# Prologue and chunk 0 of an attention and feed-forward kernel in another order

## The chip, the cores and the metric

One core of a Trainium2 chip runs the whole kernel in one launch. The metric is the device time in microseconds (us) from the start to the end of one execution, as the median of several runs.

## The reference, cut to what matters

Eight batches of 576 tokens go through attention with eight heads of 64 columns, and the result through a normalised feed-forward layer with a residue. Heads 0 to 3 are "local": a token sees the 32 tokens up to itself, within a band. Heads 4 to 7 are "strided": a token sees earlier tokens with the same position modulo 32.

```python
scores = scale * np.matmul(q, k.transpose(0, 1, 3, 2))
scores = np.where(masks[None], scores, -1e9)
attn = softmax(scores)
x = (attn @ v) as [8, 576, 512]
xn = (x - mean) / sqrt(var + 1e-6) * g_ln
out = x + np.maximum(xn @ w_ch1, 0) @ w_ch2
```

w_ch1 is 512 by 2048 and w_ch2 is 2048 by 512. Everything is float32.

## The kernel before, in words

**Chunks and steps.** The feed-forward layer runs over nine chunks of 512 tokens (chunk c is the first 512 tokens of batch c, the ninth holds the 64 left over from each batch). A chunk is 16 steps f, one for each 128 of the 2048 hidden columns. A step is F and H (12 matmuls of 128 by 512, with the weights and the input each split into a high and a low part, lines 758 and 765), hh and hl (the rectified result split, lines 770 and 775) and G (12 matmuls into the output, line 785). From chunk 1 on, attention for the next batch is mixed in between.

**Weights.** The weights arrive as float32 and are split in chunk 0, once, and stay. W:f loads step f's two weight tiles of 512 KB (lines 227 and 230). Then, for tile i of step f: sc scales (ScalarE), low or lowA takes the low bits out (VectorE or ScalarE), mg and sg put the rounded value together (VectorE), and hi (ScalarE) and lo (POOL, or VectorE with the letter D) make the high and low parts. For the first tile there stand in between: byg, a product with g_ln (POOL), add, a sum of blocks (POOL), cm, a matmul that gives column means (line 284), and cen, their subtraction (VectorE).

**Attention in the prologue and chunk 0.** A pair is two heads of one batch. Pairs 0 to 3 are batch 0, pairs 4 to 7 are batch 1; even ones are strided, odd ones local. For a pair k below 5: R:k:1 and R:k:0 load the rows of k and of q (two loads of 144 KB each; with a last field of 1, one of the two goes out on ScalarE's queue), T:k:1 and T:k:0 turn them with six transposes each (line 371), c copies the result out of PSUM (ScalarE, or VectorE as cD), S makes the scores (line 443), mask and max (VectorE), sub (POOL, or VectorE as subD), exp (ScalarE), PP turns the weights (line 499), pt copies them (ScalarE, or VectorE as ptD), V multiplies with the values (line 512), den and xo divide (VectorE), X turns the result for the layer (line 633), xh and xl split it. v:k loads the values, vs:k shifts a copy of them on POOL for a local pair. From pair 5 on, r:k loads 128-byte pieces of q and k in another layout and tp:k turns them on VectorE. Fp and Hp are step 0's F and H, one pair at a time (line 851). g loads g_ln as four rows, gt turns it on TensorE into the tile "wake", gc copies it out (lines 870 to 874). st:k stores a pair's result, xr and xs load the residue and its statistics.

**Order.** Chunk 0 and everything ahead of it is written out by hand as a list of such words, ORDER (from line 20). Each engine and each queue runs its own instructions in just that order: the last lines of the kernel add a dependency from each instruction to the one before it on its engine. So a word that waits holds up every later word of its engine. The last field of a word of TensorE is one of three PSUM buffers (room). SyncE's queue carries all loads and stores named above, but for the halves on ScalarE's queue; each load waits until an earlier one that used its semaphore is back, eight can be out. The words Z and Y are known to the function that runs the list, but the list before has none:

```python
elif op in "ZY":
    t = room(f"d{k}", buf) if op == "Y" else wake
    nc.tensor.matmul(
        t[:, 0:CH].rearrange("p (n x) -> p n x", x=P), mean.bitcast(F32R),
        mean.bitcast(F32R).unsqueeze(1).broadcast_to([P, CH // P, P]),
        start=True, stop=True)
```

They multiply a constant with itself into a buffer that nobody reads. Ahead of the list, six such products of 128 columns are run on TensorE (line 126).

The head of the list before V:4 on TensorE, without the other engines, is: T:0:0 T:0:1 T:1:1 T:1:0 S:0 S:1 T:2:1 T:2:0 PP:0 S:2 PP:1 V:0 T:3:1 gt T:3:0 X:0 S:3 T:4:1 V:1 T:4:0 cm:0 PP:2 S:4 X:1 PP:3 V:2 V:3 Fp:1 X:2 cm:1 Hp:0 Fp:0 Hp:1 X:3 Hp:2 PP:4 Fp:2 Fp:3 Hp:3 cm:2 S:5 V:4, then F:1 H:1 G:0 and so on.

Of the kernel before, what the change touches and what calls it, by code (L numbers as in the profile page):

```python
# [17 lines left out]


ORDER = """  # L20
vm R:0:1:1 R:0:0:1 R:1:1:1 T:0:0:0 R:1:0:1 T:0:1:1 cD:0:0: T:1:1:2 cD:1:1: T:1:0:0 c:0:1: S:0::2
R:2:1 R:2:0 W:0 c:1:0: v:0 mask:0 max:0 sub:0 S:1::0 T:2:1:1 T:2:0:2 c:2:1: mask:1 max:1 exp:0 R:3:1
PP:0::0 cD:2:0: low:0:0 sc:0:0 S:2::2 mg:0:0 sub:1 mask:2 exp:1 pt:0 sg:0:0 PP:1::0 pt:1 V:0::1
max:2 R:3:0 g:0 sc:0:1 sub:2 T:3:1:2 v:1 den:0 xo:0 gt:0: gc:0: T:3:0:0 low:0:1 c:3:1: c:3:0: X:0::2
R:4:1 byg:0 mg:0:1 vs:1 sg:0:1 xh:0 R:4:0 S:3::1 xl:0 hi:0:1 T:4:1:0 W:1 c:4:1: v:3 lo:0:1 mask:3
exp:2 max:3 sc:1:0 V:1::2 v:2 T:4:0:0 add:0 W:2 cm:0::1 den:1 c:4:0: xo:1 low:1:0 r:5 PP:2::2
lowA:1:1 mg:1:0 cen:0 pt:2 sub:3 sg:1:0 sc:1:1 S:4::0 X:1::2 mask:4 exp:3 mg:1:1 byg:1 xh:1 max:4
vs:3 hi:0:0 PP:3::1 pt:3 xl:1 lowA:2:0 V:2::0 V:3::2 sg:1:1 den:2 lo:0:0 Fp:1 sc:2:0 add:1 xo:2
X:2::0 cm:1::1 v:4 den:3 Hp:0 Fp:0 lowA:2:1 mg:2:0 Hp:1 xo:3 sub:4 hi:1:1 sg:2:0 cen:1 xh:2 W:3
exp:4 X:3::2 lo:1:1 byg:2 xl:2 xh:3 Hp:2 W:4 PP:4::1 Fp:2 hi:1:0 xl:3 st:1 Fp:3 add:2 pt:4 tp:5  # L30
sc:2:1 Hp:3 cm:2::0 mg:2:1 hh:0 cen:2 S:5::2 hl:0 hi:2:0 V:4::0 sg:2:1 lowA:3:0 mask:5 lo:1:0 den:4
sc:3:0 lo:2:0 mg:3:0 hi:2:1 sg:3:0 lowA:3:1 F:1 W:5 H:1 byg:3 xo:4 sc:3:1 hh:1 mg:3:1 sg:3:1 add:3
G:0 lowA:4:0 hl:1 sc:4:0 mg:4:0 sg:4:0 hi:3:1 cm:3::0 lo:2:1 cen:3 F:2 lowA:4:1 sc:4:1 hi:3:0 lo:3:1
lo:3:0 mg:4:1 lowA:5:0 H:2 sg:4:1 max:5 hh:2 X:4::0 sc:5:0 hl:2 G:1 byg:4 mg:5:0 F:3 sg:5:0 sub:5
add:4 xh:4 lowA:5:1 W:6 xl:4 sc:5:1 cm:4::0 lowA:6:0 hi:4:1 byg:5 mg:5:1 lo:4:1 sg:5:1 add:5
lowA:6:1 sc:6:0 st:2 H:3 G:2 W:7 cen:4 mg:6:0 sg:6:0 hi:4:0 hh:3 hi:5:1 byg:6 sc:6:1 hl:3 cm:5::0
exp:5 lo:4:0 F:4 mg:6:1 add:6 lowA:7:0 H:4 sg:6:1 low:7:1 sc:7:0 cen:5 cm:6::0 hi:6:1 G:3 mg:7:0
sg:7:0 cen:6 byg:7 hi:5:0 sc:7:1 mg:7:1 hh:4 r:6 W:8 sg:7:1 hl:4 st:0 hi:7:1 lowA:8:0 PP:5::0 lo:5:0
F:5 pt:5 H:5 tp:6 sc:8:0 lo:7:1 st:3 mg:8:0 S:6::0 sg:8:0 hi:6:0 hh:5 G:4 v:5 W:9 lowA:8:1 lo:6:1
add:7 loD:5:1 hl:5 sc:8:1 lo:6:0 mask:6 mg:8:1 st:4 max:6 cm:7::0 sg:8:1 hi:8:1 sc:9:0 subD:6 W:10  # L40
F:6 H:6 cen:7 loD:8:1 V:5::0 exp:6 byg:8 G:5 low:9:0 hh:6 hi:7:0 W:11 r:7 mg:9:0 sg:9:0 lowA:9:1
sc:9:1 add:8 den:5 hl:6 byg:9 lowA:10:0 xo:5 cm:8::0 mg:9:1 sg:9:1 addD:9 hi:9:1 sc:10:0 lo:7:0
cen:8 F:7 low:10:1 hi:8:0 H:7 mg:10:0 W:12 lo:9:1 sg:10:0 PP:6::0 hh:7 sc:10:1 hl:7 lo:8:0 mg:10:1
pt:6 lowA:11:1 lowA:11:0 G:6 cm:9::0 sg:10:1 sc:11:0 cen:9 mg:11:0 byg:10 F:8 hi:9:0 add:10 W:14
hi:10:1 sg:11:0 cm:10::0 cen:10 H:8 sc:11:1 mg:11:1 hi:10:0 byg:11 lo:10:1 hh:8 lo:9:0 add:11 tp:7
sg:11:1 G:7 hl:8 lowA:12:0 sc:12:0 mg:12:0 W:13 lo:10:0 S:7::0 lowA:12:1 mask:7 sg:12:0 F:9 sc:12:1
lowA:14:0 hi:11:1 max:7 H:9 cm:11::0 mg:12:1 cen:11 byg:12 hh:9 add:12 sg:12:1 lo:11:1 sc:13:0 G:8
st:5 cm:12::0 hl:9 hi:11:0 low:13:0 lo:11:0 hi:12:1 mg:13:0 lowA:13:1 sg:13:0 v:6 sc:13:1 sub:7
lowA:14:1 F:10 cen:12 H:10 mg:13:1 sg:13:1 hi:12:0 X:5::0 hh:10 W:15 xh:5 loD:12:0 G:9 xl:5 sc:14:0
hl:10 mg:14:0 hi:13:1 byg:13 exp:7 V:6::0 sg:14:0 lo:12:1 sc:14:1 xr:2 add:13 F:11 den:6 xo:6 H:11  # L50
lowA:15:1 xs:2 mg:14:1 hh:11 xr:1 lo:13:1 cm:13::0 G:10 cen:13 hi:13:0 xr:0 sg:14:1 sc:15:0
lowA:15:0 hl:11 hi:14:1 X:6::0 F:12 xs:1 xh:6 mg:15:0 byg:14 xs:0 r:8 H:12 lo:13:0 sg:15:0 sc:15:1
addD:14 G:11 lo:14:1 hh:12 xl:6 st:6 hl:12 cm:14::0 F:13 byg:15 mg:15:1 xr:3 add:15 cen:14 H:13
PP:7::0 G:12 tp:8 ptD:7 v:7 v:8 hi:14:0 hh:13 cm:15::0 lo:14:0 hl:13 F:14 H:14 sg:15:1 cen:15
hi:15:1 hi:15:0 lo:15:1 hh:14 V:7::0 r:9 lo:15:0 den:7 hl:14 G:13 xo:7 xs:3 X:7::0 F:15 H:15 xh:7
st:7 hh:15 xl:7 hl:15 G:14
"""
# [1011 lines left out]
```

## Time and profile before

| what | value |
|---|---|
| median of 3 runs | 897.91 us (897.63 to 898.39) |
| the profiled execution, its own time | 899.09 us |
| its span, first to last instruction | 897.3 us |
| TensorE busy | 880.3 us, 98% |
| VectorE, ScalarE, POOL busy | 451.0, 197.3, 143.2 us |
| mean granted clock of TensorE | 0.992 |
| moved by DMA | 103.74 MB |

A profile is one execution. PE is TensorE's matmul, DVE is VectorE, ACT is ScalarE, SPq is SyncE's queue that issues transfers. A window row gives, for a stretch of the execution, how long each engine was busy in it and the clock that TensorE was granted, as a share of full speed. A timeline row gives start, duration, engine, line of the kernel, operation and shapes; x24 means that 24 like instructions in a row were merged; the bracket gives the idle time of the engine before it and what ended it. Times count from the start of the span.

### The profile page before, as it was taken

What the parts mean: (1) busy time and instruction counts of PE and PEld (TensorE: products, weight loads), DVE (VectorE), ACT (ScalarE), POOL (GpSimd) and SP (SyncE); (2) the same over time, 40 slices, a digit from 0 to 9 for tenths busy, and PEclk for the clock granted to TensorE, in tenths of its full rate; (3) what the DMA queues carried; (4) which work ended last, traced back from release to release, by engine and by line L of the source; (5) the groups of instructions that cost most, each with busy time, mean ns of one, the idle gap of its engine ahead of it and who ended that gap; (6) DMA issues with size and microseconds to landing.
All of it is one profiled execution on the core that took longest, in us unless ns stands there. A gap on an engine that the chain in (4) does not pass through costs nothing.

```text
span 897.3 us, 18263 instructions
## 1 busy us (share of the span) xinstructions
PE 880.3 (98%) x7453; PEld 725.1 (81%) x7453; DVE 451.0 (50%) x883; ACT 197.3 (22%) x321; POOL 143.2 (16%) x178
## 2 busy tenths in 40 slices
...
GB/s 188 180 293 268 256 112 101 128 163 124 114 143 145 111 113 136 125 112 113 126 128 113 112 91 147 127 107 103 144 121 69 38 118 11 1 1 94 1 1 47
DMA packets 352683, 103.74 MB, mean 116 GB/s; under 512 B 295124, under 2 KB 344408, under 8 KB 352600
## 3 DMA queue, kind: packets, MB, share of 16 engines
...
q14 instruction: 25, 0.20, 0.1%
...
## 4 chain that ended last, share of the span: by engine, by line
PE 94%; DMA 2%; DVE 2%; issue 1%; SPq 1%; POOL 0%; ACT 0%; ACTq 0%; DVEq 0%; POOLq 0%
PE po L785 43%; PE ph L758 28%; PE ph L765 14%; PE m L512 2%; PE m L443 2%; PE s L443 1%; PE t L371 1%; PE pp L499 1%; PE av L512 1%; DMA rows<-in_q_dram 1%; DMA rows<-in_k_dram 0%; DMA pt<-pd 0%; DMA v_s<-in_v_dram 0%; SPq L399 0%; PE cm L284 0%
## 5 line engine op out<-in xcount | busy, mean ns | idle before, releaser
L785 PE MATMUL po<-w,hh 128*128 128x512 f32 x1152 | 359.0, 393 | 0.0
L775 DVE SCALAR_TENSOR_TENSOR hl<-ph,hh 128x512 fp32r<-128x512 f32 x144 | 99.4, 690 | 351.1 <-ACT hh L770 351.0
L785 PEld LDWEIGHTS po<-w,hh 128*128 128x128 f32 x1152 | 213.5, 188 | 45.3
L785 PE MATMUL po<-w,hl 128*128 128x512 f32 x576 | 224.5, 390 | 0.0
L758 PE MATMUL ph<-xh,w 128*128 128x512 f32 x572 | 224.0, 392 | 0.0
L758 PE MATMUL ph<-xl,w 128*128 128x512 f32 x572 | 222.7, 389 | 0.0
L770 ACT ACTIVATE hh<-ph 128x512 fp32r<-128x512 f32 x144 | 86.0, 597 | 465.1 <-PE ph L765 425.9
L765 PE MATMUL ph<-xh,w 128*128 128x512 f32 x572 | 153.2, 390 | 0.0
L785 PEld LDWEIGHTS po<-w,hl 128*128 128x128 f32 x576 | 108.1, 188 | 22.8
L758 PEld LDWEIGHTS ph<-xh,w 128*128 128x128 f32 x572 | 107.4, 188 | 22.3
L765 PEld LDWEIGHTS ph<-xh,w 128*128 128x128 f32 x572 | 107.2, 188 | 22.3
L758 PEld LDWEIGHTS ph<-xl,w 128*128 128x128 f32 x572 | 107.4, 188 | 22.0
L489 POOL TENSOR_TENSOR sm<-sm,mx 128x640 f32<-128x640 f32 (+1 forms) x31 | 39.4, 1270 | 343.1 <-DVE mx L484 343.1
L719 POOL TENSOR_TENSOR rs<-rs,mhalf 128x1 f32<-128x1 f32 x36 | 19.8, 550 | 357.2 <-DVE rs L718 357.1
L495 ACT ACTIVATE sm<-sm 128x648 f32<-128x648 f32 (+1 forms) x32 | 23.8, 744 | 108.2 <-POOL sm L489 108.2
L683 DVE TENSOR_TENSOR xl<-xo,xh 128x512 fp32r<-128x512 f32 x28 | 19.4, 693 | 40.0 <-ACT xh L682 40.0
L301 POOL TENSOR_TENSOR w<-r,w 128x512 fp32r<-128x512 f32 x29 | 38.0, 1320 | 8.3 <-ACT w L297 6.4
L682 ACT ACTIVATE xh<-xo 128x512 fp32r<-128x512 f32 x28 | 17.7, 632 | 69.1 <-DMA raw<-in_q_dram 24.8
L484 DVE TENSOR_REDUCE mx<-sm 128x12 f32<-128x648 f32 (+1 forms) x32 | 26.3, 823 | 2.5
L562 DVE TENSOR_TENSOR xo<-m,den 64x64 f32<-64x64 f32 (+3 forms) x120 | 27.1, 290 | 0.0
L791 DVE SCALAR_TENSOR_TENSOR x<-po,rs,x 128x512 f32<-128x512 f32 x36 | 24.6, 739 | 2.3 <-PE po L785 2.2
L714 DVE BATCH_NORM_STATS2 st<-x 128x6 f32<-128x512 f32 x36 | 24.5, 682 | 0.0
...
## 6 DMA issues: line engine op xcount, KB each, us to landing
...
raw<-in_q_dram SPq DMA_DIRECT2D x108, 72.0 KB
raw<-in_k_dram SPq DMA_DIRECT2D x108, 72.0 KB
...
```

The lines of the kernel that those rows point to most:

```text
L301: eng.tensor_tensor(out=t[:, 1], in0=self.w[i], in1=t[:, 0].bitcast(F32), op=ALU.subtract)
L443: nc.tensor.matmul(o, lhsT, rhs, start=True, stop=True, tile_position=(64 * h, pos))
L484: nc.vector.reduce_max(mx[:, :, 0:nt], sm, axis=AX.X)
L489: eng.tensor_tensor(out=sm, in0=sm, in1=mx[:, :, 0:nt].unsqueeze(3).broadcast_to([P, 2, nt, sm.shape[3]]), op=ALU.subtract)
L512: nc.tensor.matmul(at(h, t)[m * j:m * (j + 1)], self.p_cols(rows, t, j), self.v[rows, n, 0:w], start=True, stop=True, tile_position=(64 * ...
L562: nc.vector.tensor_tensor(out=xo[r, t0:t1, h0:h1].rearrange("p t h d -> p h t d"), in0=av, in1=den[r, h0:h1, t0:t1].unsqueeze(3).broadcast_to(
L758: nc.tensor.matmul(ph, w1h[:, cc], x[:, cc, :], start=(new and n == 0 and i == 0), stop=False)
L765: nc.tensor.matmul(ph, w1l[:, cc], xt[c][0][:, cc, :], start=False, stop=(cc == NCC - 1))
L770: nc.scalar.activation(out=hh, in_=ph, func=AF.Relu)
L775: nc.vector.scalar_tensor_tensor(out=hl, in0=ph, scalar=0.0, in1=hh.bitcast(F32), op0=ALU.max, op1=ALU.subtract)
L785: nc.tensor.matmul(po[i], hx[:, cs], w, start=(f == 0 and n == 0), stop=(f == NFC - 1 and n == 2))
L791: nc.vector.scalar_tensor_tensor(out=x, in0=po[i], scalar=rs, in1=x, op0=ALU.mult, op1=ALU.add)
```

## The change

Only the list ORDER is changed. Nothing else is touched. The head of it, with "-" the list before and "+" the list after:

```diff
-vm R:0:1:1 R:0:0:1 R:1:1:1 T:0:0:0 R:1:0:1 T:0:1:1 cD:0:0: T:1:1:2 cD:1:1: T:1:0:0 c:0:1: S:0::2
-R:2:1 R:2:0 W:0 c:1:0: v:0 mask:0 max:0 sub:0 S:1::0 T:2:1:1 T:2:0:2 c:2:1: mask:1 max:1 exp:0 R:3:1
-PP:0::0 cD:2:0: low:0:0 sc:0:0 S:2::2 mg:0:0 sub:1 mask:2 exp:1 pt:0 sg:0:0 PP:1::0 pt:1 V:0::1
-max:2 R:3:0 g:0 sc:0:1 sub:2 T:3:1:2 v:1 den:0 xo:0 gt:0: gc:0: T:3:0:0 low:0:1 c:3:1: c:3:0: X:0::2
-R:4:1 byg:0 mg:0:1 vs:1 sg:0:1 xh:0 R:4:0 S:3::1 xl:0 hi:0:1 T:4:1:0 W:1 c:4:1: v:3 lo:0:1 mask:3
-exp:2 max:3 sc:1:0 V:1::2 v:2 T:4:0:0 add:0 W:2 cm:0::1 den:1 c:4:0: xo:1 low:1:0 r:5 PP:2::2
...
+vm R:0:1:1 g:0 R:0:0:1 gt:0: R:1:1:1 T:0:1:1 T:0:0:2 R:1:0:1 T:1:1:0 W:0 gc:0: c:0:1: cD:0:0: c:1:1:
+S:0::1 mask:0 Y:0::0 Y:1::2 T:1:0:1 R:2:1 max:0 sub:0 lowA:0:0 sc:0:0 cD:1:0: mg:0:0 sg:0:0 S:1::0
+R:2:0 T:2:1:2 lowA:0:1 byg:0 T:2:0:1 exp:0 sc:0:1 mask:1 v:0 c:2:1: PP:0::0 mg:0:1 max:1 R:3:1 add:0
+sg:0:1 R:3:0 c:2:0: ptD:0 sub:1 hi:0:1 v:1 S:2::1 mask:2 V:0::2 T:3:1:0 exp:1 c:3:1: lo:0:1 den:0
+xo:0 PP:1::1 max:2 pt:1 T:3:0:2 X:0::0 c:3:0: cm:0::1 R:4:1 R:4:0 subD:2 exp:2 S:3::2 vs:1 cen:0 W:1
+xh:0 PP:2::1 xl:0 T:4:1:0 mask:3 max:3 hi:0:0 pt:2 v:3 low:1:0 lo:0:0 T:4:0:1 v:2 Hp:0 Fp:0 sub:3
+c:4:1: sc:1:0 c:4:0: lowA:1:1 V:1::2 mg:1:0 sg:1:0 den:1 S:4::0 xo:1 W:2 byg:1 r:5 exp:3 mask:4
...
```

On SyncE's queue the order of loads was R:0:1 R:0:0 R:1:1 R:1:0 R:2:1 R:2:0 W:0 v:0 R:3:1 R:3:0 g v:1 R:4:1 R:4:0 W:1 v:3 v:2 W:2 r:5 v:4 W:3 W:4 st:1 W:5 W:6. It becomes R:0:1 g R:0:0 R:1:1 R:1:0 W:0 R:2:1 R:2:0 v:0 R:3:1 R:3:0 v:1 R:4:1 R:4:0 W:1 v:3 v:2 W:2 r:5 v:4 W:3 W:4 W:5 W:6 st:1.

On TensorE the head becomes: gt T:0:1 T:0:0 T:1:1 S:0 Y:0 Y:1 T:1:0 S:1 T:2:1 T:2:0 PP:0 S:2 V:0 T:3:1 PP:1 T:3:0 X:0 cm:0 S:3 PP:2 T:4:1 T:4:0 Hp:0 Fp:0 V:1 S:4 X:1 PP:3 cm:1 Hp:1 V:2 V:3 X:2 Fp:1 X:3 PP:4 Hp:2 Hp:3 Fp:2 Fp:3 cm:2 S:5 V:4, then F:1 H:1 G:0 and so on.

The two products Y:0 and Y:1 are new. Over the whole list some words change engine: of the copies c one more is ScalarE's (8 instead of 7), of the low bits two more (27 instead of 25), of sub one more is VectorE's (2 instead of 1), of add one fewer (1 instead of 2). In the part after F:1 the words stand a few places earlier or later; so S:6 goes between F:5 and H:5, PP:7 between F:13 and H:13, V:7 between F:14 and H:14, V:5 behind G:5.

## Rows read from the trace of the kernel before

**Rows 1.** Windows of the whole execution: stretch, its length, each engine's busy time, granted clock
```profile
core 0: us, PE busy (x) PEld busy (x) DVE busy (x) ACT busy (x) POOL busy (x), PEclk, DMA share, GB/s
0.00:47.74 47.74, 37.18 (x828) 31.35 (x828) 34.61 (x72) 26.79 (x40) 29.98 (x57) 0.89 0.97 191
...
30.89:46.76 15.87, 14.86 (x309) 12.06 (x309) 13.01 (x24) 12.50 (x21) 11.60 (x12) 0.81 0.76 162
47.74:143.15 95.41, 95.41 (x764) 78.14 (x760) 83.63 (x138) 58.55 (x101) 65.10 (x66) 1.00 0.86 222
```

**Rows 2.** Timeline of PE: start, duration, engine, line, operation, shapes, count, [idle before <- releaser]
```profile
24.64 0.69 PE L371 MATMUL t<-ident,rows 96*128 96x96 f32 x6 [0.29 <-DMA rows<-in_k_dram]
...
26.90 0.47 PE L371 MATMUL t<-ident,rows 96*128 96x96 f32 x3
30.89 0.74 PE L371 MATMUL t<-ident,rows 96*128 96x96 f32 x3 [3.53 <-issue]
...
44.77 0.38 PE L284 MATMUL cm<-bsum,mean 128*128 128x128 f32 x2
45.63 1.03 PE L443 MATMUL s<-kt_l,qt_l 64*32 64x64 f32 x80 [0.48 <-DVE kt_l L414]
46.76 1.05 PE L512 MATMUL av<-v_s,pt 54*64 54x65 f32 x48
47.74 0.50 PE L758 MATMUL ph<-xh,w 128*128 128x512 f32 x1
```

**Rows 3.** Windows around PE's gaps, columns as in rows 1
```profile
14.40:16.06 1.66, 0.00 (x1) 0.01 (x1) 1.56 (x4) 1.62 (x3) 1.18 (x2) 1.00 0.91 141
16.40:19.70 3.30, 3.30 (x58) 2.74 (x56) 2.46 (x5) 1.57 (x3) 0.57 (x1) 0.51 1.22 186
...
30.40:36.80 6.40, 5.91 (x68) 5.25 (x68) 3.56 (x6) 4.55 (x7) 3.17 (x3) 0.50 0.86 222
36.80:46.76 9.96, 8.95 (x242) 6.80 (x241) 9.86 (x20) 7.95 (x15) 8.43 (x10) 0.99 0.67 119
...
45.00:47.74 2.74, 2.16 (x131) 1.84 (x129) 2.74 (x5) 1.20 (x2) 1.09 (x2) 1.00 0.92 302
```

**Rows 4.** Timeline of SyncE's queue from 0 to 60 us
```profile
4.67 0.86 SPq L364 DMA_DIRECT2D rows<-in_k_dram  x2
...
7.79 1.21 SPq L227 DMA_DIRECT2D s<-in_moe_w_ch_dram  x1
...
17.01 0.60 SPq L870 DMA_DIRECT2D grow<-in_moe_g_ln_dram  x1
...
31.29 0.40 SPq L227 DMA_DIRECT2D s<-in_moe_w_ch_dram  x1
...
41.31 2.38 SPq L399 DMA_DIRECT2D v_s<-in_v_dram  x6
```

**Rows 5.** DMA: 36 to 46 us in 40 slices, then packets of 45 to 46, 46 to 47
```profile
GB/s 235 199 161 130 120 96 80 93 23 10 43 183 145 22 64 170 51 7 10 5 0 81 172 83 181 124 65 82 108 153 127 129 132 157 127 104 91 86 105 296
...
DMA packets 162, 0.14 MB, mean 145 GB/s; under 512 B 27, under 2 KB 162, under 8 KB 162
...
DMA packets 346, 0.37 MB, mean 369 GB/s; under 512 B 7, under 2 KB 339, under 8 KB 346
```

**Rows 6.** Timelines of ScalarE and VectorE
```profile
27.67 0.63 ACT L247 ACTIVATE p<-s 128x512 f32<-128x512 f32 x1 [0.52 <-DMA s<-in_moe_w_ch_dram]
...
15.47 1.23 DVE L382 COPY qt_s<-t 128x576 f32<-128x576 f32 x1
16.53 0.72 DVE L257 TENSOR_SCALAR s<-s 128x512 uint32<-128x512 uint32 x1
...
44.73 0.76 DVE L414 STREAM_TRANSPOSE kt_l<-raw 128x576 f32<-128x576 f32 x1
...
78.94 0.83 DVE L489 TENSOR_TENSOR sm<-sm,mx 128x648 f32<-128x648 f32 x1
```

**Rows 7.** DMA queues from 27 to 31 us
```profile
q8 instruction: 1, 0.02, 2.0%
```

More of the change, by code (lines that the diff above doesn't have):

```diff
@@ L26 @@
-exp:2 max:3 sc:1:0 V:1::2 v:2 T:4:0:0 add:0 W:2 cm:0::1 den:1 c:4:0: xo:1 low:1:0 r:5 PP:2::2
[L27 to L55, printed above, removed]
@@ L56 @@
-st:7 hh:15 xl:7 hl:15 G:14
+vm R:0:1:1 g:0 R:0:0:1 gt:0: R:1:1:1 T:0:1:1 T:0:0:2 R:1:0:1 T:1:1:0 W:0 gc:0: c:0:1: cD:0:0: c:1:1:
[3 more added lines that the diff above has]
+xo:0 PP:1::1 max:2 pt:1 T:3:0:2 X:0::0 c:3:0: cm:0::1 R:4:1 R:4:0 subD:2 exp:2 S:3::2 vs:1 cen:0 W:1
@@ new lines @@
+xh:0 PP:2::1 xl:0 T:4:1:0 mask:3 max:3 hi:0:0 pt:2 v:3 low:1:0 lo:0:0 T:4:0:1 v:2 Hp:0 Fp:0 sub:3
+c:4:1: sc:1:0 c:4:0: lowA:1:1 V:1::2 mg:1:0 sg:1:0 den:1 S:4::0 xo:1 W:2 byg:1 r:5 exp:3 mask:4
+X:1::2 add:1 PP:3::0 sc:1:1 mg:1:1 cm:1::1 xh:1 vs:3 max:4 pt:3 Hp:1 sg:1:1 sub:4 cen:1 V:2::0
+hi:1:1 V:3::1 sc:2:0 xl:1 lowA:2:0 den:2 xo:2 mg:2:0 lo:1:1 X:2::2 exp:4 v:4 den:3 Fp:1 hi:1:0 xo:3
+xh:2 sg:2:0 lo:1:0 W:3 lowA:2:1 byg:2 X:3::1 PP:4::0 xh:3 xl:2 add:2 sc:2:1 W:4 xl:3 Hp:2 Hp:3 pt:4
+Fp:2 Fp:3 mg:2:1 tp:5 hh:0 cm:2::0 S:5::1 sg:2:1 cen:2 hl:0 W:5 V:4::0 mask:5 F:1 hi:2:1 den:4 H:1
```

25 lines of the change are left out of this document (added).

## The prediction

> **What bounds the kernel now.** I read the windows of the profile first, by stage. From 47.74 us, where TensorE (PE) starts the first full step of chunk 0 (F:1), to 143.15, where chunk 1 begins, PE is busy 100% at a clock of 1.00 [rows 1]. The change keeps every matmul behind F:1 and only permutes them inside chunk 0, so this part can lose by a new wait but has no idle time to give back. What is open to gain is the prologue: 37.18 us busy of 47.74 [rows 1]. The order of words before V:4 holds the same set in both orders, apart from the two products Y, so the end moves by as much as F:1 moves, plus any new stall or slow clock behind it.
>
> The second view is the timeline of PE. It shows the idle times: 1.66 us before PP:0 [rows 3], 3.53 in the middle of the six transposes of T:4:0 (three run at 26.90, three at 30.89, all on the same rows, released by "issue", so not by data), 0.48 before S:5 [rows 2]. The tempting reading is that these waits, and the two stretches at half clock behind two of them (0.51 from 16.40 to 19.70, 0.50 from 30.40 to 36.80, [rows 3]), are the prize. The third view, SyncE's queue with the DMA rows, speaks against it. W:2 was issued at 31.29, then r:5, then v:4 from 41.31 for 2.38 us [rows 4]. V:4 reads v:4's rows, which go in pieces under 512 B; of these 27 stand between 45 and 46 us and 7 between 46 and 47, where W:3's larger pieces already dominate [rows 5]. So the last of v:4 lands at about 46.2 to 46.5, and V:4 ran at 46.76 [rows 2]: the prologue ends 0.3 to 0.6 us behind its loads. Upstream it is alike: T:4:1 waited 0.29 us for R:4 [rows 2], ScalarE 0.52 us for W:1, up to 27.67 [rows 6].
>
> **The change, part by part.**
> *Loads.* SyncE's order changes in two places: g (2 KB, at 17.01) goes to second place, and W:0's two issues (from 7.79) go ahead of R:2's four (from 4.67) [rows 4]. From v:0 on to W:4 the list is the same, and the bytes ahead of each load are the same but for g. g saves the queue 0.60 us in the middle [rows 4] and takes one place among the first loads, so half of R:1's q rows goes out later, on ScalarE's queue. It still stands behind loads in flight, and T:1:0, its reader, now comes after S:0, so I cost it at nothing; without that cover T:1:0, S:1 and T:2 slip, and T:4:1's load still ends the slip. R:2 lands later by W:0's 1 MB: at the rate of such pieces, 0.37 MB in the microsecond from 46 [rows 5], 2.8 us. So T:2 slips by up to that. What is late next is S:2, but V:0, T:3 and T:4 behind it wait for loads that have not moved (T:4:1 at 24.64), so the delay ends there. Price for v:4's landing: 0, between -0.6 (g's issue) and +0.6 (the slot).
>
> *The two products* of 512 columns: the first matmul of F:1, of that size, took 0.50 us [rows 2], so 1.0 us for both at full clock, up to 2.0 at half. They stand between S:0 and T:1:0, ahead of the wait for T:4:1, so they cost nothing at the end; without that cover 2 us.
>
> *Engines.* One copy of pair 2's rows moves from VectorE to ScalarE, both low-bit operations of step 0 likewise; sub:2 moves from POOL and pt:0 from ScalarE to VectorE. VectorE, which was busy 9.86 of the 9.96 us before V:4 [rows 3], gives away 1.2 + 2 x 0.7 us and takes 2 x 0.8 (rows of such forms: 1.23, 0.72 and 0.83, [rows 6]; pt:0 is put at sub's), so 1.0 us less. It transposed r:5's keys at 44.73 [rows 6], the release of S:5. r:5's last issue lies before 41.31; v:4's last, at 43.7, is back 2.5 to 2.8 us later, so by the same delay r:5 is in by 43.4 to 43.9, or sooner, and S:5, one 0.76 us transpose later, can go to about 44.2, 1.4 us earlier. That helps only up to V:4's data. ScalarE has more to do ahead of S:4: the copy c:4:0 stands behind sc:1:0, which waits for W:1, as it did at 27.67; S:4 comes at about 29.7, behind W:1 by one scaling and one copy, well ahead of V:4.
>
> *PE between T:4:0 and V:4.* Before: 14.86 us busy from 30.89 to 46.76 [rows 1], of it 5.91 at half clock [rows 3]; at full clock that is 14.86 - 2.95 = 11.9. After, cm:0, PP:2 and half of T:4:0 are done earlier (1.2 us) and V:1 comes later (1.0): 11.7. T:4:0 needs R:4's last half, between 24.64 and 26.90 by rows 2; I take 26.9 for its end. So 11.7 us of work stand in the 19.3 us up to 46.2: PE will idle some 7.6 us there, waiting for W:1, v:2, W:2, r:5 and v:4, whose order is unchanged. The stall at T:4:0 is not saved, it is spread.
>
> *Sum.* F:1 goes from 47.74 to about 47.3: -0.4 (bounds -0.6 and 0). Then the clock. After 1.66 us without a matmul the granted clock was 0.51 (the 1.2 GHz level) for the next 3.3 us; after 3.53 us it was 0.50 for 6.4 us [rows 3]. In the new order PE has S:5 alone (1.03 us) between cm:2 and V:4 at 46.2. cm:2 ran at 44.77 [rows 2]; I put it 2 us earlier, 42.8, an estimate: VectorE, which feeds it, has 1.0 us less to do and PE's gap of 3.53 us is no longer in front. That leaves 2.4 us idle, in two pieces, just ahead of the dense steps. So I expect one half-clock stretch to reach into V:4 and F:1. A whole one of 3.3 us costs 1.65; if it starts up to 1.3 us before V:4, 1.0. I take 1.3. Sum: -0.4 + 1.3 = +0.9 us, on the profiled execution 897.3 to 898.2 of span. That execution took 899.09 us in all, 1.18 above the median of the three runs, 897.91; the difference goes on top of the median: 898.8.
>
> A short gap did not have this effect: behind 0.48 us at 45.63 [rows 2] the clock stayed at 1.00 [rows 1, 3]. The Trainium skill, "TensorE: Matmul & The Clock Gate", section "HAM oscillation — how this bites in real kernels", says that a TensorE that waits for DMA between bursts of matmuls is throttled again and starts the next burst cold, at half rate. That rule speaks against an order that turns one gap into several; taken for every gap here it would give the third rival below, 900.7, where the rows of short gaps alone would give the first, 897.5.
>
> **The rivals.**
> *Clock holds:* the idle time falls in pieces too short, or S:5 keeps the clock up. For it: the 0.48 us gap left it at 1.00. Against it: the 1.66 us gap. -0.4: 897.5.
> *Loads come sooner (faster):* between 38.0 and 41.25 ten of thirteen slices of the GB/s row stand at 64 or less, although k rows of r:5 and all of v:4 were still to come [rows 5]. If that hole, 2.5 us, follows from what else sits in the queues at that moment (an instruction packet, say, like that of [rows 7]), another timing may close it. VectorE and PE are ready by then, S:5 and V:4 move up by 2.5, F:1 to 45.2: 895.4. Against it: the loads in front are the same.
> *Clock stays down (slower):* as from 30.40 to 36.80 [rows 3]: 6.4 us at half, 3.2 lost if all of it falls on V:4 and the dense steps, less 0.4: +2.8, 900.7. It decides if the 2.4 us idle ahead of V:4 act like the gap of 3.53 us rather than like that of 1.66; they lie between.
> *Stall at the same place in PE's program:* one packet of the instruction queue stands in the stretch of the 3.53 us gap [rows 7]. If it was the release, the gap returns at the same count of instructions, now in V:1, up to 30.9. S:4 then comes at 31, and V:2 behind it waits for v:2 until about 33.5 anyway (its issue ends at 31.29, [rows 4]). It changes nothing at the end, so it is part of the forecast.
>
> **How the numbers follow.** About 0.2%, 1.8 us, is what a measurement can tell. Forecast (one slow stretch, 898.8): 0.40, range of its own 898.3 to 899.6 from the bounds (-0.6 + 1.0 and 0 + 1.65). Clock holds (897.5): 0.22, also within 0.2%. Loads sooner (895.4): 0.18, faster. Clock stays down (900.7): 0.16, slower. A new wait inside chunk 0, where VectorE is busy 83.63 of 95.41 us [rows 1] and a permuted word could be late: 0.04, slower, 901 and more. So faster 0.18, same 0.62, slower 0.20. The range reaches from the case of sooner loads to a little above that of the clock that stays down, 895.3 to 901.0.
>
> **What would show it.** Right: T:4:1 waits for R:4 at 24 to 25 us; no 3.5 us gap, but several gaps of 0.5 to 1.7 us from 27 to 46; S:5 near 44, V:4 near 46.3, F:1 near 47.3; granted clock near 0.5 somewhere from 44 to 50; 100% busy from F:1 on. Wrong: v:4's small pieces ending before 45 or F:1 before 46.5 (loads were not the bound), or idle PE between F:1 and chunk 1.

## The result, and the profile after

The new order is slower: 904.23 us (median of four runs, 902.63 to 905.39) against 897.85 for the kernel before (897.63 to 898.39), a ratio of 1.0069 with a 95% interval of 1.0051 to 1.0086. That lies outside the predicted range. The profiled execution took 902.63 us, with a span of 900.82; the profiled one of before had a span of 897.3. So the traces show 3.5 of the 6.4 us; the other three runs of the kernel after have no trace.

The windows of the kernel after (columns as in rows 1) say where to look. F:1 starts at 47.14, chunk 1 at 147.85:

```profile
0.00:47.14 47.14, 35.58 (x830) 29.39 (x830) 33.92 (x72) 28.98 (x43) 29.20 (x56) 0.96 0.99 189
47.14:80.00 32.86, 32.54 (x197) 25.86 (x193) 31.48 (x48) 25.47 (x44) 27.79 (x30) 1.00 0.98 292
80.00:110.00 30.00, 30.00 (x293) 24.50 (x292) 26.64 (x42) 20.59 (x35) 24.49 (x26) 1.00 0.92 261
110.00:147.85 37.85, 34.35 (x277) 27.63 (x276) 24.41 (x45) 12.97 (x22) 12.38 (x15) 1.00 0.57 106
```

The prologue ends 0.60 us sooner, near the 0.4 of the forecast. From F:1 on, where PE was busy 95.41 of 95.41 us [rows 1], it now idles 3.50 us behind 110 and 0.32 ahead of 80, at a granted clock of 1.00. From F:1 to chunk 1 it takes 100.71 us, 5.30 more than before; 3.82 of them are these idle times, the rest stands between matmuls, in time that counts as busy. No slow clock is in this: the half-clock stretch lay earlier, from 40 to 44 us (0.55, 0.50, 0.50 and 0.74 in its four microseconds), behind a gap of 2.02 us, and was over by 44. The rows that answer to rows 2 and 3, from the timeline of PE and from windows:

```profile
26.36 1.21 PE L371 MATMUL t<-ident,rows 96*128 96x96 f32 x12 [0.86 <-DVE xl L664]
29.53 0.41 PE L512 MATMUL av<-v_l,pt 64*32 64x65 f32 x18 [0.46 <-issue]
...
40.57 1.09 PE L633 MATMUL px<-ident,xo 128*128 128x128 f32 x4 [2.02 <-DVE xo L562]
...
44.48 0.38 PE L284 MATMUL cm<-bsum,mean 128*128 128x128 f32 x2
45.01 1.04 PE L443 MATMUL s<-kt_l,qt_l 64*32 64x64 f32 x80 [0.15 <-DVE kt_l L414]
46.18 1.03 PE L512 MATMUL av<-v_s,pt 54*64 54x65 f32 x48
47.14 0.50 PE L758 MATMUL ph<-xh,w 128*128 128x512 f32 x1
```
```profile
42.00:43.00 1.00, 1.00 (x6) 1.00 (x5) 0.75 (x3) 0.85 (x3) 0.87 (x2) 0.50 0.46 82
43.00:44.00 1.00, 1.00 (x4) 0.77 (x4) 1.00 (x3) 0.77 (x1) 0.46 (x1) 0.74 0.60 133
44.00:47.14 3.14, 2.85 (x134) 2.33 (x132) 3.14 (x6) 1.77 (x3) 0.81 (x1) 1.00 0.87 240
```

Now the idle time behind 110, in four timelines of the kernel after: PE, then VectorE, SyncE's queue and POOL. Read from the top, the waits of F:13 (126.89) and F:14 (135.12) go back to rows below them; that of V:6 (112.36) has another cause, shown further down.

```profile
112.36 1.03 PE L512 MATMUL av<-v_s,pt 54*64 54x65 f32 x48 [0.67 <-DMA x<-xdl]
...
126.89 0.50 PE L758 MATMUL ph<-xh,w 128*128 128x512 f32 x1 [1.15 <-DVE hl L775]
...
135.12 0.50 PE L758 MATMUL ph<-xh,w 128*128 128x512 f32 x1 [1.68 <-DVE hl L775]
```
```profile
125.14 0.69 DVE L714 BATCH_NORM_STATS2 st<-x 128x6 f32<-128x512 f32 x1 [1.78 <-DMA x<-xds]
...
126.16 0.68 DVE L775 SCALAR_TENSOR_TENSOR hl<-ph,hh 128x512 fp32r<-128x512 f32 x1
...
130.74 1.26 DVE L418 STREAM_TRANSPOSE qt_s<-raw 128x576 f32<-128x576 f32 x1 [2.30 <-DMA raw<-in_q_dram]
132.69 1.26 DVE L418 STREAM_TRANSPOSE kt_s<-raw 128x576 f32<-128x576 f32 x1 [0.69 <-DMA raw<-in_k_dram]
...
134.40 0.67 DVE L775 SCALAR_TENSOR_TENSOR hl<-ph,hh 128x512 fp32r<-128x512 f32 x1
```
```profile
110.39 0.33 SPq L707 DMA_DIRECT2D x<-xdl  x1
110.76 0.53 SPq L709 DMA_DIRECT2D x<-xds  x1
120.39 0.31 SPq L707 DMA_DIRECT2D x<-xdl  x1
...
121.37 2.85 SPq L399 DMA_DIRECT2D v_s<-in_v_dram  x6
124.32 1.29 SPq L580 DMA_DIRECT2D xds<-xo  x2
125.65 2.67 SPq L354 DMA_DIRECT2D raw<-in_q_dram  x4
128.36 2.48 SPq L354 DMA_DIRECT2D raw<-in_k_dram  x4
```
```profile
118.16 0.94 POOL L719 TENSOR_TENSOR rs<-rs,mhalf 128x1 f32<-128x1 f32 x1 [7.79 <-DVE rs L718]
119.06 1.30 POOL L301 TENSOR_TENSOR w<-r,w 128x512 fp32r<-128x512 f32 x1
```

F:13 (126.89) and F:14 (135.12) wait for hl:12 and hl:13 on VectorE, because their PSUM tile ph has one buffer. VectorE had stood waiting for data just ahead of each: for xr:0's rows (xs:0, L714) and for r:8's (tp:8, L418). Both loads are late on SyncE's queue, which issues nothing from 111.29 to 120.39: xr:0 stands there and waits for one of the seven buffers that it shares with the split weights (L266, L701). lo:13:1 on POOL frees it at 120.36, and r:8 goes out behind it at 125.65. In the kernel before, r:8 stood ahead of the last x load, which waited five microseconds as well, with nothing urgent behind it:

```profile
110.27 0.33 SPq L707 DMA_DIRECT2D x<-xdl  x1
...
111.21 3.00 SPq L354 DMA_DIRECT2D raw<-in_q_dram  x4
114.25 2.12 SPq L354 DMA_DIRECT2D raw<-in_k_dram  x4
116.47 0.80 SPq L580 DMA_DIRECT2D xds<-xo  x2
122.25 0.34 SPq L707 DMA_DIRECT2D x<-xdl  x1
```

The Trainium skill, "Perfetto Trace Analysis", section "What "DMA-bound" means", tells a bound by the issuing engine from its track being solid with DMA slices. By that sign this queue would not be suspected: the rows here show it late where its track is empty, for nine microseconds, because its first entry waits.

That gave **theory 1**: xr:0 ahead of r:8 on SyncE costs what F:13 and F:14 wait. **Theory 2**: VectorE's and POOL's work in its new order is late by itself (addD:13, xs:1). **Theory 3**: the new prologue or its clock costs the time.

### The profile page after: what moved, and what is told of

It reads as the page before. It is cut to its first block, busy times and chain, and to the rows that moved or that the text cites. A ratio compares the mean times of both kernels' runs of the same rounds, so it can differ in the third digit from the quotient of the medians.

```text
span 900.8 us, 18274 instructions
## 1 busy us (share of the span) xinstructions
PE 880.1 (98%) x7455; PEld 723.0 (80%) x7455; DVE 449.6 (50%) x879; ACT 200.1 (22%) x324; POOL 142.0 (16%) x179
## 4 chain that ended last, share of the span: by engine, by line
PE 90%; SPq 4%; DMA 3%; issue 1%; DVE 1%; POOL 1%; ACTq 0%; POOLq 0%; DVEq 0%
PE po L785 42%; PE ph L758 28%; PE ph L765 14%; PE m L512 2%; PE m L443 2%; SPq L354 1%; SPq L399 1%; DMA rows<-in_q_dram 1%; SPq L364 1%; DMA rows<-in_k_dram 1%; POOL w L301 1%; DMA x<-xds 0%; DMA s<-in_moe_w_ch_dram 0%; PE cm L284 0%; DVE x L791 0%
## 5 line engine op out<-in xcount | busy, mean ns | idle before, releaser
L714 DVE BATCH_NORM_STATS2 st<-x 128x6 f32<-128x512 f32 x36 | 24.6, 682 | 1.8 <-DMA x<-xds 1.8
```

The lines of the kernel that those rows point to most:

```text
L714: nc.vector.bn_stats(st, x)
```

## The experiments

The columns of this table are worked out from the timelines of PE: the start of a step in that run's profiled execution less its start in the profiled execution of the kernel before (F:1 47.74, F:2 53.46, F:6 78.63, F:10 104.82, F:11 111.85, F:12 118.28, F:13 124.16, F:14 130.47, chunk 1 143.15). What counts is the change from column to column. The ratios are each run's own, of all its executions against the kernel before on the same chip.

| run | F:1 | F:2 | F:6 | F:10 | F:11 | F:12 | F:13 | F:14 | chunk 1 | ratio (95%) |
|---|---|---|---|---|---|---|---|---|---|---|
| after | -0.60 | 0.07 | 0.69 | 0.68 | 1.47 | 1.54 | 2.74 | 4.66 | 4.70 | 1.0069 (1.0051-1.0086) |
| after, once more | -1.92 | -1.26 | -0.63 | -0.63 | 0.17 | 0.23 | 0.98 | 3.38 | 3.42 | 1.0041 (1.0028-1.0055) |
| chunk 0 alone | -1.44 | -0.42 | 0.18 | 0.16 | 0.96 | 1.04 | 2.28 | 3.78 | 3.79 | 1.0060 (1.0048-1.0072) |
| prologue alone | -1.49 | -0.20 | -0.20 | -0.22 | -0.22 | -0.25 | -0.23 | -0.23 | -0.23 | 1.0006 (0.9996-1.0016) |
| xr:0 late | 1.75 | 2.41 | 3.04 | 3.03 | 3.83 | 3.92 | 3.72 | 3.68 | 3.70 | 1.0009 (0.9999-1.0019) |
| lo:13:1 first | -0.55 | 0.19 | 0.77 | 0.74 | 1.53 | 1.62 | 1.42 | 3.68 | 5.25 | 1.0039 (1.0024-1.0054) |
| r:8 first | -2.10 | -1.00 | -1.00 | -1.01 | -0.21 | -0.13 | 1.44 | 1.43 | 1.45 | 1.0012 (1.0003-1.0021) |
| xr:0 late, no addD:13 | -0.79 | -0.14 | 0.48 | 0.48 | 0.44 | 0.45 | 0.26 | 0.22 | 0.24 | 0.9996 (0.9987-1.0005) |
| the same, two cm waits | -2.31 | -1.88 | -0.48 | -0.46 | -0.50 | -0.50 | -0.69 | -0.73 | -0.75 | 1.0004 (0.9995-1.0013) |
| before, xr:3 ahead of r:8 | 0.84 | 1.15 | 1.15 | 1.14 | 1.14 | 1.11 | 3.23 | 3.22 | 3.22 | 1.0024 (1.0014-1.0034) |

**Prologue or chunk 0.** Two kernels splice the orders at F:1. The first keeps the new prologue (its lines against those of the kernel after):

```diff
-Fp:2 Fp:3 mg:2:1 tp:5 hh:0 cm:2::0 S:5::1 sg:2:1 cen:2 hl:0 W:5 V:4::0 mask:5 F:1 hi:2:1 den:4 H:1
+Fp:2 Fp:3 mg:2:1 tp:5 hh:0 cm:2::0 S:5::1 sg:2:1 cen:2 hl:0 W:5 V:4::0 mask:5 st:1 hi:2:0 lowA:3:0
+den:4 sc:3:0 lo:2:0 mg:3:0 hi:2:1 sg:3:0 lowA:3:1 F:1 H:1 byg:3 xo:4 sc:3:1 hh:1 mg:3:1 sg:3:1 add:3
...
```

> The prologue of the kernel after up to F:1, with the rest of chunk 0 in the order of the kernel before. If the loss lies in the rest of chunk 0 (theories 1 and 2), only the 0.6 us gained at F:1 remains: 897 to 898.5, with PE busy over 99.5% from F:1 to chunk 1. If the prologue (clock, late words carried over) costs the time (theory 3): 902 to 905.

The second keeps the old one (against the kernel before):

```diff
-sc:3:0 lo:2:0 mg:3:0 hi:2:1 sg:3:0 lowA:3:1 F:1 W:5 H:1 byg:3 xo:4 sc:3:1 hh:1 mg:3:1 sg:3:1 add:3
+sc:3:0 lo:2:0 mg:3:0 hi:2:1 sg:3:0 lowA:3:1 W:5 F:1 H:1 W:6 lo:2:1 sc:3:1 xo:4 mg:3:1 G:0 hh:1 byg:3
...
```

> The prologue of the kernel before up to F:1, with the rest of chunk 0 in the order of the kernel after. Theories 1 and 2: the loss of 4 to 5 us inside chunk 0 remains and the 0.6 us at F:1 is not there, 902 to 905. Theory 3 (the prologue costs the time): 897 to 899.

Measured: 898.66 us with the new prologue alone (ratio 1.0006; 0.2 us above the range expected), 903.44 with the new chunk 0 alone (1.0060). Theory 3 falls. The order from F:1 on costs all of it, and the new prologue gains nothing that can be measured: the 0.2 us left of F:1's lead is within the interval.

**xr:0 out of the way.**

```diff
-hi:13:0 loD:13:0 hh:11 hi:14:1 hl:11 X:6::0 mg:15:0 xr:2 sg:15:0 F:12 H:12 xr:0 add:14 xh:6 v:8
-sc:15:1 xs:3 xl:6 mg:15:1 lo:14:1 hh:12 byg:15 xs:0 G:11 st:6 hl:12 xs:2 cm:14::0 cen:14 add:15 F:13
-r:8 v:7 hi:14:0 tp:8 PP:7::0 lo:14:0 H:13 hh:13 sg:15:1 pt:7 G:12 hl:13 r:9 cm:15::0 hi:15:1 F:14
+hi:13:0 loD:13:0 hh:11 hi:14:1 hl:11 X:6::0 mg:15:0 xr:2 sg:15:0 F:12 H:12 add:14 xh:6 v:8 sc:15:1
+xs:3 xl:6 mg:15:1 lo:14:1 hh:12 byg:15 G:11 st:6 hl:12 xs:2 cm:14::0 cen:14 add:15 F:13 r:8 v:7 xr:0
-cen:15 hi:15:0 loD:15:0 V:7::0 H:14 den:7 G:13 xo:7 lo:15:1 X:7::0 hh:14 hl:14 F:15 st:7 xh:7 H:15
+hi:14:0 tp:8 PP:7::0 lo:14:0 H:13 hh:13 sg:15:1 pt:7 G:12 hl:13 r:9 cm:15::0 hi:15:1 F:14 cen:15
+hi:15:0 loD:15:0 V:7::0 H:14 den:7 G:13 xo:7 xs:0 lo:15:1 X:7::0 hh:14 hl:14 F:15 st:7 xh:7 H:15
```

> The kernel after with two words moved: the x load xr:0 goes behind v:7 on SyncE's list (so r:8 and v:7 no longer stand behind it), its scaling xs:0 behind xo:7. If xr:0, waiting for a buffer, holds the queue and so the loads r:8 and v:7 for the next chunk (theory 1), the waits ahead of F:13 (1.15 us) and F:14 (1.68 us) go, PE idles under 1 us between 110 us and chunk 1, and the time falls by about 3 us to 900 to 902. If the moved VectorE work (addD:13 and its like) is itself too late (theory 2), F:13 and F:14 wait as before and the time stays at 903 to 905. If the prologue or the clock costs the time (theory 3): unchanged, 903 to 905.

Measured: 899.19 us, ratio 1.0009; F:12 to chunk 1 loses nothing (3.92, then 3.70). Theory 1 holds; the time is even below its range, by 0.8 us. The profiled execution was the slowest of the eleven (901.50), its F:1 at 49.48.

**What it waited for, freed sooner.**

```diff
-sc:14:1 xo:6 lowA:15:1 xr:3 cm:13::0 H:11 mg:14:1 sg:14:1 cen:13 G:10 xs:1 lo:13:1 sc:15:0 byg:14
+sc:14:1 xo:6 lowA:15:1 xr:3 cm:13::0 H:11 mg:14:1 sg:14:1 cen:13 G:10 lo:13:1 xs:1 sc:15:0 byg:14
```

> The kernel after with one word moved: lo:13:1, which frees the buffer that xr:0 waits for, goes ahead of xs:1 in the list, so POOL does it before the power of xs:1 that made it wait from 110 to 118 us. Theory 1: xr:0 is issued at about 112 us in place of 120.4, r:8 by about 118, the waits ahead of F:13 and F:14 shrink to under 0.7 us together, 900 to 902. Theory 2 (VectorE's own order is too late): no change over 1 us, 903 to 905. Theory 3 (prologue or clock): 903 to 905.

Measured: 901.55 us, ratio 1.0039, no better than the kernel after in its second measurement (1.0041, below). The time lies in the range that theory 1 gave, but it did not come about in that way: POOL did finish lo:13:1 seven microseconds sooner, but xr:0 left at 118.77 and r:8 at 124.19. The waits of the queue, the timelines of POOL and VectorE and of the queue itself show why:

```profile
SPq L707 <- DVE w L301: 7.3, 1, 7.3
```
```profile
111.97 1.28 POOL L301 TENSOR_TENSOR w<-r,w 128x512 fp32r<-128x512 f32 x1 [1.55 <-ACT w L297]
```
```profile
118.06 0.68 DVE L301 TENSOR_TENSOR w<-r,w 128x512 fp32r<-128x512 f32 x1
```
```profile
118.77 0.32 SPq L707 DMA_DIRECT2D x<-xdl  x1
```

The other half of step 13 (loD:13:0, on VectorE) now frees the buffer, and is done at 118.74. POOL's 7.79 us of idle time was not the root: a second gate opened only 1.6 us before the first had.

F:13 no longer waits in this profile, but F:14 still does, and behind its gap the granted clock fell to the 1.2 GHz level, which no other profile shows between F:2 and chunk 1. F:14 to chunk 1 lost 1.6 us more by it. In the timeline of PE and in a window:

```profile
134.14 0.65 PE L758 MATMUL ph<-xh,w 128*128 128x512 f32 x1 [2.05 <-DVE hl L775]
```
```profile
134.00:138.00 4.00, 3.86 (x41) 2.65 (x42) 1.43 (x3) 0.85 (x2) 1.28 (x1) 0.57 0.71 115
```

**One word: r:8 ahead of xr:0**, and the kernel after once more beside it.

```diff
-hi:13:0 loD:13:0 hh:11 hi:14:1 hl:11 X:6::0 mg:15:0 xr:2 sg:15:0 F:12 H:12 xr:0 add:14 xh:6 v:8
+hi:13:0 loD:13:0 hh:11 hi:14:1 hl:11 X:6::0 mg:15:0 xr:2 sg:15:0 F:12 H:12 r:8 xr:0 add:14 xh:6 v:8
...
-r:8 v:7 hi:14:0 tp:8 PP:7::0 lo:14:0 H:13 hh:13 sg:15:1 pt:7 G:12 hl:13 r:9 cm:15::0 hi:15:1 F:14
+v:7 hi:14:0 tp:8 PP:7::0 lo:14:0 H:13 hh:13 sg:15:1 pt:7 G:12 hl:13 r:9 cm:15::0 hi:15:1 F:14 cen:15
...
```

> The kernel after with one word moved: r:8 goes ahead of xr:0 on SyncE's list, xr:0 and xs:0 stay where they are. If the late rows of r:8 are all of the loss in the tail, F:13 and F:14 wait no more and the time is near that of the run with xr:0 late (899 to 900). If xs:0, which waits on VectorE for xr:0's data ahead of hl:12, costs by itself, F:13 still waits 1 us or more and F:14 does not: 900 to 902. If neither counts: 903 to 905.

> The kernel after, as it is, beside the others on one chip and profiled once more. Its ratio should stand at 1.005 to 1.008 again. The waits of the tail (F:12 to F:15 lost 3.1 us in the first profile) should stand at 2.5 us or more in this one too, and F:10 to F:11 at 0.8; F:1 may differ by a microsecond between profiles, with the landing of v:4.

Measured on the same chip: 902.84 us for the kernel after (its ratio below the range expected for it, 1.0041), 899.73 with r:8 first (1.0012). One word of the order is worth 3.1 us by these medians. From F:12 to chunk 1, where it acts, the two profiles lose 3.19 and 1.58 us. In the timelines of the run with r:8 first, the queue and VectorE:

```profile
109.65 2.77 SPq L354 DMA_DIRECT2D raw<-in_q_dram  x4
...
118.68 0.34 SPq L707 DMA_DIRECT2D x<-xdl  x1
```
```profile
123.85 0.69 DVE L714 BATCH_NORM_STATS2 st<-x 128x6 f32<-128x512 f32 x1 [2.20 <-DMA x<-xds]
...
127.06 1.25 DVE L418 STREAM_TRANSPOSE qt_s<-raw 128x576 f32<-128x576 f32 x1
```

VectorE no longer waits for r:8 (127.06), and F:13 to F:14 loses nothing, where the kernel after lost 1.92 and 2.40. xr:0 is as late as ever, so xs:0 still waits for its rows, hl:12 stands behind it, and F:13 still waits: 1.57 in the table. So both of the expected parts stand in the trace, r:8's the larger; the time is in the range that was given for r:8 alone. What xs:0's wait is worth in time isn't shown: the ratios of this run and of the one with xr:0 late (1.0012 and 1.0009) can't be told apart.

**The cause put into the kernel before.**

```diff
-lowA:15:0 hl:11 hi:14:1 X:6::0 F:12 xs:1 xh:6 mg:15:0 byg:14 xs:0 r:8 H:12 lo:13:0 sg:15:0 sc:15:1
-addD:14 G:11 lo:14:1 hh:12 xl:6 st:6 hl:12 cm:14::0 F:13 byg:15 mg:15:1 xr:3 add:15 cen:14 H:13
+lowA:15:0 hl:11 hi:14:1 X:6::0 F:12 xs:1 xh:6 mg:15:0 byg:14 xs:0 xr:3 r:8 H:12 lo:13:0 sg:15:0
+sc:15:1 addD:14 G:11 lo:14:1 hh:12 xl:6 st:6 hl:12 cm:14::0 F:13 byg:15 mg:15:1 add:15 cen:14 H:13
```

> The cost by itself, in the kernel before: its last x load, xr:3, which was issued at 122.25 us behind r:8, goes one place ahead of r:8; nothing else moves. Theory 1 (a load that waits for a buffer holds every load behind it on SyncE): r:8 is issued at about 122 to 123 us in place of 111.21, VectorE waits for its rows as in the kernel after, PE idles 1.5 to 4 us ahead of F:14 and the time rises by 1.5 to 4 us, ratio 1.002 to 1.004. Rival (the queue has slack; the loss belongs to the new order of VectorE's and POOL's work): under 0.5 us.

Measured: 901.31 us, ratio 1.0024, so 2.6 us (2.1 in the table). The size is as expected, the way is only half of it. r:8 did go out late, at 119.09. But the wait that showed came ahead of F:13, and on another resource:

```profile
123.19 0.69 DVE L267 SCALAR_TENSOR_TENSOR r<-s,p 128x512 uint32<-128x512 uint32 x1 [1.92 <-POOL w L301]
```

A half of the split weights on VectorE waits for a buffer that POOL frees. Why it must: xr:3 now takes one of the seven shared buffers one turn sooner than the weights that used to get it. That is read from the order of the buffers, not tried by itself. By the time VectorE reaches r:8's rows they are there, so what r:8 alone would have cost in this order isn't seen.

**The sums of step 13.** On top of the run with xr:0 late:

```diff
-sc:13:1 cen:12 X:5::0 lo:11:0 byg:13 mg:13:1 lowA:14:1 hi:12:0 hh:10 sub:7 addD:13 xh:5 sg:13:1
+sc:13:1 cen:12 X:5::0 lo:11:0 byg:13 mg:13:1 lowA:14:1 hi:12:0 hh:10 sub:7 add:13 xh:5 sg:13:1
```

> The kernel with xr:0 late, and the sums of step 13 (addD:13, 1.47 and 1.27 us on VectorE) moved to POOL, where the kernel before had them. If they delay xl:5, and by that the buffer that V:6 and then F:11 wait for, the 0.8 us lost from F:10 to F:11 comes back: ratio about 0.0009 lower than that of the run with xr:0 late, F:11 less F:10 at 7.0 us in place of 7.8. If something else makes V:6 late: no change.

Measured: 897.98 us, ratio 0.9996, and F:10 to F:11 loses nothing in place of 0.80. In the kernel after, V:6 waits 0.67 us at 112.36 (above; the row names an x load, the profile of the same kernel once more names xl, with 0.66). It needs the PSUM tile that xl:5 frees, and xl:5 stands behind the two sums; the first two rows here are of the kernel after, the third of this run:

```profile
109.24 1.27 DVE L280 TENSOR_TENSOR bsum<-bsum 128x128 f32<-128x128 f32 x1
...
111.63 0.68 DVE L664 TENSOR_TENSOR xl<-px,xh 128x512 fp32r<-128x512 f32 x1
```
```profile
109.60 0.68 DVE L664 TENSOR_TENSOR xl<-px,xh 128x512 fp32r<-128x512 f32 x1
```

So theory 2 holds for 0.8 to 1.2 us. With these words back, the order takes as long as the kernel before.

**The 0.6 us between F:2 and F:6.**

```diff
-F:3 xh:4 lo:3:0 add:4 mg:5:0 sg:5:0 hi:4:1 xl:4 cm:4::0 lo:4:1 sc:5:1 mg:5:1 exp:5 byg:5 sg:5:1
+F:3 xh:4 lo:3:0 add:4 mg:5:0 xl:4 sg:5:0 hi:4:1 cm:4::0 lo:4:1 sc:5:1 mg:5:1 exp:5 byg:5 sg:5:1
...
-byg:6 sc:6:1 lowA:7:0 mg:6:1 sg:6:1 F:4 cen:5 add:6 cm:6::0 hi:5:1 sc:7:0 mg:7:0 sg:7:0 hi:6:1 H:4
+byg:6 sc:6:1 lowA:7:0 mg:6:1 sg:6:1 F:4 cen:5 add:6 hi:5:1 sc:7:0 mg:7:0 sg:7:0 hi:6:1 H:4 cm:6::0
```

> The order with xr:0 late and the sums of step 13 on POOL, and two words more: xl:4 ahead of sg:5:0, cm:6 behind H:4. If the two losses of 0.3 us (ahead of H:3 and of H:4) come from a small matmul cm that waits there for its PSUM buffer, which VectorE frees (xl:4, cen:5), both go: F:6 less F:2 at 25.2 us as in the kernel before, in place of 25.8, and the time 0.6 us less than without them, ratio 0.999. If they come from the fill of PE's pipe by the form of the order: no change.

Measured: 898.22 us, ratio 1.0004: a miss. The two losses did go (F:3 to H:3 takes 1.95 us, as in the kernel before, where the run without the edit took 2.30; F:4 to H:4 1.98, where it took 2.38). But with xl:4 put ahead VectorE comes late to an hl, PE waits for that instead, and F:2 to F:6 takes 26.56 us, longer than without the edit:

```profile
64.66 0.50 PE L758 MATMUL ph<-xh,w 128*128 128x512 f32 x1 [0.73 <-DVE hl L775]
```

VectorE was busy 31.48 of the 32.86 us from F:1 to 80 in the kernel after: there a word moved up on it can push another past its time.

**Is it v:4 that the prologue ends behind?** One half of v:4 on ScalarE's queue, in three orders: the prologue alone, the run just above, the kernel before.

```diff
-            dma = nc.sync.dma_start
             for h in range(2):
+                dma = (nc.scalar if h and self.k == 4 else nc.sync).dma_start
                 src = v[self.b, self.h0 + h]
```

> The new prologue with chunk 0 in the old order (the run named prologue alone), and one half of v:4, three of its six issues, on ScalarE's queue in place of SyncE's. If the prologue ends behind its loads (the prediction's step), F:1 starts about 1 us earlier than in the run with the prologue alone, W:3 is issued 1.2 us earlier, and the time falls by 0.5 to 1.2 us against it, to 897.5 to 898.2 beside a before of 898.6. If F:1 hangs on VectorE or on TensorE's own order, there is no change; if the chunk's steps are held by W:3's scaling, F:1 gains and F:2 does not.

> The run before this one with one half of v:4 on ScalarE's queue as well. If both effects are real they add: 1.2 to 1.8 us under the order with xr:0 late and the sums on POOL, ratio 0.998. If W:3 holds the first steps, F:1 moves up and F:2 stays within 0.3 us.

> The kernel before, whose chunk 0 has no wait, with one half of v:4 on ScalarE's queue. If SyncE's time for issuing (the last of v:4 leaves it at 43.7 us) sets F:1, F:1 and the time fall by about 1 us, ratio 0.9985 to 0.9995. If ScalarE, busy 7.4 of 8 us ahead of it, gets late by the issues, or F:1 hangs on W:2 or VectorE: no change or a little slower.

Measured: 910.34, 914.42 and 910.94 us, ratios 1.0131, 1.0176 and 1.0141; F:1 came 12.04, 15.83 and 13.71 us late. That is nothing like what was expected. ScalarE (here of the first) held its three issues back, and everything behind them; the last row is the window from 40 to 48:

```profile
37.34 0.74 ACT L495 ACTIVATE sm<-sm 128x648 f32<-128x648 f32 x1
48.58 3.05 ACTq L399 DMA_DIRECT2D v_s<-in_v_dram  x3
51.67 0.63 ACT L297 ACTIVATE w<-r 128x512 fp32r<-128x512 f32 x1 [13.59 <-DMA s<-in_moe_w_ch_dram]
```
```profile
40.00:48.00 8.00, 0.79 (x8) 0.55 (x6) 0.00 (x0) 0.00 (x0) 0.00 (x0) 0.65 0.87 248
```

In eight microseconds VectorE, ScalarE and POOL do nothing at all and PE 0.79 us. The row puts it to weight loads that SyncE issued; why the issue had to wait for those isn't settled. A candidate, not tried: in the trace the loads of both queues use the same eight semaphores, so an issue on ScalarE can have to wait for a load that SyncE issued. As a test of the prediction's step it is inconclusive, since ScalarE's other work was held as well.

## Why the prediction was wrong

**The step that failed** stands in its first paragraph: chunk 0 "can lose by a new wait but has no idle time to give back". From that the permuted words behind F:1 were priced at nothing, and "a new wait inside chunk 0" got a chance of 0.04. The list of loads was compared from v:0 to W:4, no further. But the change moves loads past each other on SyncE in the tail of chunk 0 too: r:8, second behind xr:0 in the new order, stood ahead of the last x load before. It was a place where a load with slack (the x rows are read in chunk 1, though xs:0 stood early) could stop one without. Rows to price it were there in the trace of before: the wait of five microseconds in front of 122.25, and a PE that was busy 100% [rows 1]. Measured by one word: 3.1 us. VectorE's sums (addD:13) were a second such place, 0.8 us in the traces and 0.0013 in the ratios (1.0009 and 0.9996, each against its own runs of before, with intervals that overlap). Both are the last rival, on the side and at the size it was given ("901 and more"); its chance was what was wrong. Beside these the new order loses about 0.6 us from F:2 to F:6, though not in the profile with r:8 first, where the same words stood behind an F:1 at half clock; and it loses 0.7 from F:1 to F:2, as follows.

**F:1** was put at 47.3 and came at 47.14. The gain of 0.6 went by F:2 (0.07 in the table): cm:3 waits for POOL's sums, and in this profile these go back to W:3's data, for which ScalarE waited up to 48.00 (47.81 in the kernel before). But the loads did not set this limit. Five profiles of this order lose 0.65 to 0.74 us from F:1 to F:2, with F:1 anywhere from 45.81 to 49.48, and in the latest of them (xr:0 late) ScalarE scales W:3 without a wait. So the loss goes with the words behind F:1, which the prediction had priced at nothing. One of them is low:3:0 on VectorE, ahead of the sums; ScalarE did that work in the order before (lowA:3:0). It was not tried by itself. A row each of PE and VectorE in the kernel after, and of ScalarE with xr:0 late:

```profile
53.22 0.49 PE L284 MATMUL cm<-bsum,mean 128*128 128x128 f32 x2 [0.18 <-POOL bsum L280]
```
```profile
48.00 1.16 DVE L257 TENSOR_SCALAR s<-s 128x512 uint32<-128x512 uint32 x1
```
```profile
49.04 0.65 ACT L247 ACTIVATE p<-s 128x512 f32<-128x512 f32 x1
```

**The clock.** The stretch at the 1.2 GHz level did not reach F:1 in the kernel after; the 1.3 us priced for it fell away. It rested on 2.4 us of idle PE ahead of V:4, with cm:2 put at 42.8. cm:2 came at 44.48, PE idled 0.15 us behind it, and the long gap stood earlier, ahead of X:3 (2.02 us). The mechanism was seen elsewhere. In the run with the new prologue alone PE idled three times between 41.9 and 45.1 us (0.25, 0.66 and 0.58), and F:1 to H:1 took 3.22 us, where the kernel before took 1.95:

```profile
46.25:49.48 3.23, 3.23 (x12) 2.56 (x10) 2.25 (x5) 2.74 (x5) 0.40 (x2) 0.57 1.03 370
```

That is 1.27 us, the size that was taken, and the run's median shows no net loss. With r:8 first it came again (1.10 us). In both, a third idle piece, V:4's wait for v:4, followed two that other executions had too; in the kernel after, once more, those two alone (0.24 and 0.66) left the clock at 1.00. So the term was of the right size and a matter of the single execution. The Trainium skill's rule weighed in the prediction ("TensorE: Matmul & The Clock Gate", section "HAM oscillation — how this bites in real kernels") agrees with the gap of 2.02 us above, with that of 2.05 with lo:13:1 first and with these two runs. It does not hold for every gap here: in the kernel after, once more, PE idled 2.16 us ahead of F:14, and the clock stayed at 1.00.

**Loads as the bound.** V:4 waited for v:4 itself in three of the eleven profiles without the split (0.58, 0.77 and 0.15 us); in the others, before and after among them, it stood right behind S:5, which waited for VectorE's transpose of r:5. "The prologue ends 0.3 to 0.6 us behind its loads" was therefore too simple: two chains end within a microsecond of each other. In the kernel after VectorE began this transpose at 43.53, straight behind its own words, without a wait for r:5. Nor did T:4:1 wait for its load at 24 to 25 us: it stood until 26.36 behind VectorE's xl. Two slips in the working do not change this: by the delay that the prediction took itself, r:5 is in by 43.8 to 44.1 and S:5 can go at 44.6 to 44.9 (it was put at 44.2 and came at 45.01), and the bounds of F:1 left out the +0.6 that the loads had been given. The 3.53 us stall did go, spread over PE as the prediction said, and was worth nothing at the end, also as it said.

Open: why the first measurement shows 6.4 us and the second 3.7 (ratio 1.0041). In the first, the profiled execution of the kernel before stood 1.2 us above its median and that of the kernel after 1.6 below its own, which is what lies between 6.4 and the 3.5 of the traces; the executions at the medians have no trace. Two things that move from execution to execution can be seen in the profiles: the time behind the start of chunk 1, from 752.8 to 754.4 us in the eleven without the split, and a slow clock like that of lo:13:1 first. The mean granted clock of the other three (0.998, 0.996 and 0.995, in the order of 905.39, 904.38 and 904.07 us; 0.998 in the profiled one) doesn't follow the time.
